# A narrower last part and smaller pieces: splitting the last tile's W4 groups 512/128 and the weight loads in a gated attention/MLP kernel

## The chip, the cores and the metric

The kernel runs on one core of a Trainium2 chip. The metric is the device time of one execution in microseconds (us); the profile's span is about 1.8 us shorter than it. Slow runs (one execution of the kernel before took 305.26 us) are left out of every comparison. Ratios are the mean time of one kernel's fast runs over that of the other's fast runs of the same rounds on the same chip, so not quite the ratio of the medians quoted beside them; each comes with a 95% interval.

The engines are called as in the profile: PE is the matrix engine, PEld its weight loads, DVE is VectorE, ACT is ScalarE, POOL is GpSimd, SP issues the DMAs; a q after the name is the engine's instruction queue.

## The reference, cut to what matters

```python
# x: (1, 2048, 640) bf16; B_w3: (640, 1728), B_w4: (1728, 640)
def reference(...):
    g = sigmoid((x * gate_w).sum(-1, keepdims=True))
    a = linear_attention(x, A_wqkv) @ A_wo            # 32 heads of 20
    x1 = x + shifted(gelu(layernorm(x) @ B_w1)) @ B_w2
    b = x1 + gelu(layernorm(x1) @ B_w3) @ B_w4
    return g * a + (1 - g) * b                        # (1, 2048, 640) bf16
```

The last step of the program is the W4 product of the last 512 rows: four chunks of 128 rows, each 640 output columns wide and 1728 deep (13 full groups of 128 and a rest of 64).

## The kernel before

An accumulator tile ("pair") is two parts of 512 float32 columns, here called banks; there are four such tiles. In W4 each chunk takes one pair. Its 640 columns are cut at 256: half 0 in the first bank, half 1 (384 columns) in the second, side by side so that VectorE can read 640 columns at once.

```python
TS = 512; LT = TS // 2; D = 640; FF = 13; NT = 4

def pair():
    return ps.tile([P, 2, 512], F32, name="pp")       # pool of 4

def w4_dst(cc, pts, hf):
    return (pts[cc][:, 0, TS - LT:TS], 0, LT) if hf == 0 else (pts[cc][:, 1, 0:D - LT], LT, D)

def w4_mm(t, cc, pts, hf, start):                     # 13 matmuls, one group
    dst, a, b = w4_dst(cc, pts, hf)
    for fc in range(FF):
        nc.tensor.matmul(dst, lhsT=st[t]["h2"][:, ...], rhs=w4_sb[:, fc, a:b], start=..., stop=...)

def w4_part(t, cc, pts, hf):                          # one half: VectorE, then a store
    src, a, b = w4_dst(cc, pts, hf)
    oc = outp.tile([P, D], BF16, name="oc")
    nc.vector.scalar_tensor_tensor(oc[:, a:b], src, omg[:, c:c + 1], st[t]["x1"][cc][:, a:b], ...)
    nc.sync.dma_start(out2[c * P:(c + 1) * P, a:b], oc[:, a:b])

def w4_tile(t):
    ...                                               # chunks 0 and 2, then the rest rows of all four
    for cc in (0, 2):
        w4_out(t, cc, pts[cc])                        # a whole chunk: VectorE 640 columns, one store
    last = t == NT - 1
    for cc, hf in ((3, 1), (1, 0), (1, 1), (3, 0)) if last else ((1, 0), (1, 1), (3, 0), (3, 1)):
        ...
        w4_mm(t, cc, pts, hf, False)
        if last and cc == 3:
            w4_part(t, cc, pts, hf)
        elif hf == 1:
            w4_out(t, cc, pts[cc])
```

The weights that the change touches come early in the program, all from SP's queue, and GpSimd gathers 128 columns of w1 from four places into `w1x`:

```python
sp.dma_start(wv_sb[:], wqkv_v[:, :, 2 * D:3 * D])
sp.dma_start(w1_sb[:], B_w1.rearrange("(c p) f -> p c f", p=P))
...                                                   # wo, w2
sp.dma_start(w3_sb[:], B_w3.rearrange("(c p) f -> p c f", p=P))
...
for g in range(4):
    nc.gpsimd.tensor_copy(w1x[:, :, 32 * g:32 * (g + 1)], w1_sb[:, :, CG * g + P:CG * (g + 1)])
```

The framework adds the waits on semaphores by itself. DMAs take their semaphores in turn out of a set of eight, so how many DMAs a program has decides which one the last store gets.

## Time and profile before

| | |
|---|---|
| time, fast runs | 266.3 and 266.91 us, profiled run 266.17 us |
| span of the profiled run | 264.4 us |
| PE busy | 259.7 us (98%) |
| last matmul's end to the end of the span | 3.70 us |

The first two parts of the page that matter are the busy times and the chain that ended last, of the kernel before (the chain's shares are by engine):

```profile
PE 259.7 (98%) x1744; PEld 162.2 (61%) x1744; DVE 139.3 (53%) x270; ACT 85.1 (32%) x126; POOL 20.2 (8%) x55
...
PE 91%; SPq 3%; DMA 3%; ACT 1%; issue 0%; DVE 0%
```

PE is the limit, and it has no pauses to win back except at the two ends. This is the timeline of the last 12 us (start, duration, engine, source line, operation, count; in brackets the idle time just before it and what ended it):

```profile
253.49 7.24 PE L479 MATMUL pp<-w_sb,h 128*128 128x384 bf16 x52
...
259.35 0.89 DVE L495 SCALAR_TENSOR_TENSOR oc<-pp,omg,x 128x640 bf16<-128x640 f32 x1 [2.60 <-PE pp L479]
260.26 0.33 SPq L497 DMA_DIRECT2D out_dram<-oc  x1
260.77 0.48 DVE L503 SCALAR_TENSOR_TENSOR oc<-pp,omg,x 128x256 bf16<-128x256 f32 x1 [0.53 <-PE pp L479]
261.28 0.33 SPq L505 DMA_DIRECT2D out_dram<-oc  x1
```

The 52 matmuls run without a break. After them stand one VectorE instruction, one store, and then 1.6 us from the store's issue to its landing, as the list of DMA issues of the last 14 us shows for the kernel before (what, from where, count, size, median us to landing):

```profile
out_dram<-oc SPq DMA_DIRECT2D x3, 160.0 KB, 1.8
out_dram<-oc SPq DMA_DIRECT2D x1, 96.0 KB, 1.6
out_dram<-oc SPq DMA_DIRECT2D x1, 64.0 KB, 1.6
```

The rest belongs to the program's closing instructions, which the views of engine work leave out. The view of their source line has them, here for the kernel before (engine, operation, count: min/median/max ns, first and last start):

```profile
L591 SPq EVENT_SEMAPHORE  x7: 17/28/28, 262.9 to 264.4; - x7
...
L591 POOLq DRAIN  x3: 78/171/1149, 203.7 to 264.0; - x3
L591 SPq DRAIN  x3: 7/7/13, 263.2 to 263.5; - x3
...
L591 POOLq EVENT_SEMAPHORE_RANGE_CLEAR  x1: 96/96/96, 263.6 to 263.6; - x1
```

SP passes its first closing check at 262.9 us, when the store has landed, and only then reaches its drain at 263.2 us. GpSimd clears the semaphores at 263.6 us (0.1 us), but its last drain starts at 264.0 us.

### The profile page before, as it was taken

Reading aid. Unit: us, or ns where it says so; the run is one execution under the profiler, and the core shown is the slowest. Engines: PE = TensorE matmul, PEld = TensorE weight load, DVE = VectorE, ACT = ScalarE, POOL = GpSimd, SP = SyncE. Lnnn points to the kernel's source line nnn. Section 1 sums busy time; section 2 is a strip of 40 time slices with the busy share of each in tenths; the row PEclk is TensorE's granted clock in tenths of the full one; section 3 lists DMA queues with packets and bytes.
Section 4 is the critical chain, followed back from the end, with each engine's and each line's share of the span. In section 5 each row is a group of like instructions: output and inputs, shape, how many; then the busy total and the mean of one; then the engine's idle time right before and its main releaser. Section 6 shows DMA issues by size and latency. Waiting matters only on the chain.

```text
span 264.4 us, 4255 instructions
## 1 busy us (share of the span) xinstructions
PE 259.7 (98%) x1744; PEld 162.2 (61%) x1744; DVE 139.3 (53%) x270; ACT 85.1 (32%) x126; POOL 20.2 (8%) x55
## 2 busy tenths in 40 slices
PE   8999999999999999999999999999999999999994
PEld 4767555788755644555667555667565667455762
DVE  1788688899858588955403464503455313112132
ACT  1555444321165636622502212312131422233000
POOL 7100010012300140001000001000001000000000
PEclk9999999999999999999999999999999999999999
DMA  7999978015673727600132000042000041100011
GB/s 202 184 211 365 377 222 318 0 43 121 128 92 68 78 51 193 207 0 2 25 74 77 25 0 2 0 99 75 26 0 2 1 99 58 44 0 2 0 59 40
DMA packets 46093, 23.61 MB, mean 89 GB/s; under 512 B 35451, under 2 KB 45435, under 8 KB 46075
## 3 DMA queue, kind: packets, MB, share of 16 engines
q1 hardware_dynamic: 45632, 22.86, 34.0%
q10 hardware_dynamic: 442, 0.49, 0.5%
q8 instruction: 13, 0.21, 0.3%
q14 instruction: 6, 0.04, 0.1%
HBM read 12.21 MB, written 2.62 MB: 56 GB/s over the span
## 4 chain that ended last, share of the span: by engine, by line
PE 91%; SPq 3%; DMA 3%; ACT 1%; issue 0%; DVE 0%
PE pp L479 22%; PE pp L460 21%; PE pp L307 8%; PE pp L413 8%; PE pp L444 8%; PE pp L341 8%; PE pp L232 8%; PE pp L190 4%; SPq L121 3%; DMA xT<-in_A_x_dram 3%; PE pp L468 1%; PE pp L488 1%; ACT m_sb L381 1%; PE pp L360 1%; PE pp L247 0%; SPq L124 0%
## 5 line engine op out<-in xcount | busy, mean ns | idle before, releaser
L460 PE MATMUL pp<-lnxT,w_sb 128*128 128x512 bf16 x260 | 60.4, 379 | 0.0
L479 PE MATMUL pp<-w_sb,h 128*128 128x256 bf16 (+1 forms) x416 | 57.9, 299 | 0.0
L462 ACT ACTIVATE h<-pp 128x1024 bf16<-128x1024 f32 (+1 forms) x28 | 26.9, 961 | 82.2 <-PE pp L460 82.2
L479 PEld LDWEIGHTS <-h 128*128 128x128 bf16 x416 | 40.3, 98 | 16.6 <-issue 1.1
L460 PEld LDWEIGHTS <-w_sb 128*128 128x128 bf16 x260 | 25.4, 98 | 26.8
L495 DVE SCALAR_TENSOR_TENSOR oc<-pp,omg,x 128x640 bf16<-128x640 f32 x15 | 12.9, 882 | 44.0 <-ACT h2x L471 21.3
L447 DVE SCALAR_TENSOR_TENSOR x<-pp,gate,x 128x640 f32<-128x640 f32 x16 | 13.9, 868 | 29.4 <-PE pp L444 29.4
L416 DVE TENSOR_TENSOR x<-pp,x_sb 128x640 f32<-128x640 f32 x16 | 13.1, 820 | 22.6 <-PE pp L413 22.6
L182 ACT ACTIVATE e<-pp 128x640 bf16<-128x640 f32 (+1 forms) x26 | 21.5, 826 | 9.6 <-PE pp L232 9.6
L444 PE MATMUL pp<-m_sb,pqT 128*128 128x320 bf16 x160 | 24.3, 299 | 0.0
L413 PE MATMUL pp<-w_sb,hsT 128*128 128x320 bf16 x160 | 23.9, 299 | 0.1
L190 PE MATMUL pp<-wk_sb,xT 128*128 128x320 bf16 (+1 forms) x160 | 22.6, 300 | 0.1
L307 PE MATMUL pp<-x_sb,pk 128*128 128x320 bf16 (+1 forms) x160 | 22.3, 300 | 0.0
L232 PE MATMUL pp<-xT,hsT 128*128 128x512 bf16 x100 | 21.7, 379 | 0.0
L307 PEld LDWEIGHTS <-pk 128*128 128x128 bf16 x160 | 18.8, 117 | 3.5
L413 PEld LDWEIGHTS <-hsT 128*128 128x128 bf16 x160 | 15.6, 98 | 8.2 <-issue 0.2
L444 PEld LDWEIGHTS <-pqT 128*128 128x128 bf16 x160 | 15.7, 98 | 7.7
L190 PEld LDWEIGHTS <-xT 128*128 128x128 bf16 x160 | 15.4, 98 | 6.4 <-DMA xT<-in_A_x_dram 0.6
L341 PE MATMUL pp<-lnxT,w_sb 128*128 128x512 bf16 x80 | 17.9, 379 | 0.0
L232 PEld LDWEIGHTS <-hsT 128*128 128x128 bf16 x100 | 11.8, 118 | 9.7
L277 POOL TENSOR_SCALAR rstd<-mv 128x4 f32<-128x4 f32 (+1 forms) x11 | 3.4, 313 | 156.5 <-DVE mv L283 156.5
L184 DVE SCALAR_TENSOR_TENSOR pk<-pp,e 128x640 bf16<-128x640 f32 x16 | 13.2, 825 | 1.7
(77 smaller groups left out, 191.6 us busy)
## 6 DMA issues: line engine op xcount, KB each, us to landing
out_dram<-oc SPq DMA_DIRECT2D x15, 160.0 KB, 1.8
w_sb<-in_B_w_dram SPq DMA_DIRECT2D x1, 2160.0 KB, 8.4
w_sb<-in_B_w_dram SPq DMA_DIRECT2D x1, 2080.0 KB, 10.0
x_sb<-in_A_x_dram SPq DMA_DIRECT2D x2, 640.0 KB, 10.7
x_sb<-in_A_x_dram SPq DMA_DIRECT2D x1, 1120.0 KB, 8.2
wo_sb<-in_A_wo_dram SPq DMA_DIRECT2D x6, 160.0 KB, 8.3
hsT<-in_A_wqkv_dram SPq DMA_DIRECT2D x1, 800.0 KB, 5.7
m_sb<-in_A_wqkv_dram SPq DMA_DIRECT2D x1, 800.0 KB, 11.5
```

The lines of the kernel that those rows point to most:

```text
L182: nc.scalar.activation(ev, src, ACT.Exp)
L184: nc.vector.scalar_tensor_tensor(dst, src, 0.0, ev, op0=ALU.max, op1=ALU.add)
L190: nc.tensor.matmul(pt[:, hf, 0:n], lhsT=xT[:, dc, c * P:(c + 1) * P], rhs=wk_sb[:, dc, hf * HD:hf * HD + n], start=(dc == 0), stop=(dc == ...
L232: nc.tensor.matmul(pt[:, t % 2, :], lhsT=wq_sb[:, dc, :].rearrange("p (m j) -> p j m", j=DC)[:, j], rhs=xT[:, dc, t * TS:(t + 1) * TS], st ...
L307: nc.tensor.matmul(pt[:, hf, 0:HD + hf], lhsT=w, rhs=x_sb[:, c, hf * HD:(hf + 1) * HD + hf], start=(c == 0), stop=(c == NCH - 1))
L341: nc.tensor.matmul(pt[:, i, :], lhsT=w, rhs=lnxT[t][:, dc, :], start=(dc == 0), stop=(dc == DC - 1))
L413: nc.tensor.matmul(pt[:, hf, 0:HD], lhsT=hsT[:, fc, 2 + c * P:2 + (c + 1) * P], rhs=w2_sb[:, fc, hf * HD:(hf + 1) * HD], start=(fc == 0), ...
L444: nc.tensor.matmul(pt[:, hf, 0:HD], lhsT=pqT[:, j, c * P:(c + 1) * P], rhs=m_sb[:, j, hf * HD:(hf + 1) * HD], start=(j == 0), stop=(j == D ...
L447: nc.vector.scalar_tensor_tensor(x1, pt[:, :, 0:HD], gate[:, c:c + 1], x1, op0=ALU.mult, op1=ALU.add)
L460: nc.tensor.matmul(pt[:, k, :], lhsT=w3_sb[:, dc, fc * P:(fc + 1) * P], rhs=lnT[:, dc, :], start=(dc == 0), stop=(dc == DC - 1))
L462: nc.scalar.activation(h2[:, 2 * i * TS:(2 * i + n) * TS], pt[:].rearrange("p h e -> p (h e)")[:, 0:n * TS], ACT.Gelu_apprx_tanh)
L479: nc.tensor.matmul(dst, lhsT=st[t]["h2"][:, fc * TS + cc * P:fc * TS + (cc + 1) * P], rhs=w4_sb[:, fc, a:b], start=start and fc == 0, stop ...
```

## The change

Its intent: the last VectorE instruction and the last store are to be narrower (128 columns in place of 256), and the early weight loads and copies are to be in finer pieces, so that their readers can start sooner. The groups of chunks 1 and 3 in the last tile become 512 and 128 columns, both wide ones first, and every group gets its own VectorE instruction and store.

```diff
-    sp.dma_start(wv_sb[:], wqkv_v[:, :, 2 * D:3 * D])
-    sp.dma_start(w1_sb[:], B_w1.rearrange("(c p) f -> p c f", p=P))
+    for a, b in ((0, 2), (2, DC)):
+        sp.dma_start(wv_sb[:, a:b, :], wqkv_v[:, a:b, 2 * D:3 * D])
+    for a, b in ((0, 2), (2, DC)):
+        sp.dma_start(w1_sb[:, a:b, :], B_w1[a * P:b * P, :].rearrange("(c p) f -> p c f", p=P))
 ...                                                  # w3 in two pieces in the same way
-    for g in range(4):
-        nc.gpsimd.tensor_copy(w1x[:, :, 32 * g:32 * (g + 1)], w1_sb[:, :, CG * g + P:CG * (g + 1)])
+    for a, b in ((0, 1), (1, 2), (2, 3), (3, DC)):
+        for g in range(4):
+            nc.gpsimd.tensor_copy(w1x[:, a:b, 32 * g:32 * (g + 1)], w1_sb[:, a:b, CG * g + P:CG * (g + 1)])
 ...
-    def w4_dst(cc, pts, hf):
-        return (pts[cc][:, 0, TS - LT:TS], 0, LT) if hf == 0 else (pts[cc][:, 1, 0:D - LT], LT, D)
+    def w4_dst(t, cc, pts, hf):
+        n = D - TS if t == NT - 1 and cc % 2 else LT
+        return (pts[cc][:, 0, TS - n:TS], 0, n) if hf == 0 else (pts[cc][:, 1, 0:D - n], n, D)
 ...                                                  # w4_part: both parts of a chunk share one oc tile
-        for cc, hf in ((3, 1), (1, 0), (1, 1), (3, 0)) if last else ((1, 0), (1, 1), (3, 0), (3, 1)):
+        for cc, hf in ((3, 1), (1, 1), (1, 0), (3, 0)) if last else ((1, 0), (1, 1), (3, 0), (3, 1)):
 ...
-            if last and cc == 3:
+            if last:
                 w4_part(t, cc, pts, hf)
```

More of the change, by code (lines that the diff above doesn't have):

```diff
@@ L145 @@
         sp.dma_start(w2_sb[32 * g:32 * (g + 1), 4, :], B_w2[CG * g + P:CG * (g + 1), :])
-    sp.dma_start(w3_sb[:], B_w3.rearrange("(c p) f -> p c f", p=P))
+    for a, b in ((0, 2), (2, DC)):
+        sp.dma_start(w3_sb[:, a:b, :], B_w3[a * P:b * P, :].rearrange("(c p) f -> p c f", p=P))
     nc.gpsimd.memset(mhalf[:], -0.5)
@@ L471, in w3_rest @@
         nc.scalar.activation(st[t]["h2x"][:], dst, ACT.Gelu_apprx_tanh)
-    def w4_dst(cc, pts, hf):
-        return (pts[cc][:, 0, TS - LT:TS], 0, LT) if hf == 0 else (pts[cc][:, 1, 0:D - LT], LT, D)
+    def w4_dst(t, cc, pts, hf):
+        n = D - TS if t == NT - 1 and cc % 2 else LT
+        return (pts[cc][:, 0, TS - n:TS], 0, n) if hf == 0 else (pts[cc][:, 1, 0:D - n], n, D)
     def w4_mm(t, cc, pts, hf, start):
-        dst, a, b = w4_dst(cc, pts, hf)
+        dst, a, b = w4_dst(t, cc, pts, hf)
         for fc in range(FF):
@@ L486, in w4_rest @@
                     rows = slice(FR * v, FR * (v + 1))
-                    dst, a, b = w4_dst(u + 2 * v, pts, hf)
+                    dst, a, b = w4_dst(t, u + 2 * v, pts, hf)
                     nc.tensor.matmul(dst, lhsT=st[t]["h2x"][rows, u * P:(u + 1) * P],
@@ L497, in w4_out @@
         nc.sync.dma_start(out2[c * P:(c + 1) * P, :], oc[:])
+    ocs = {}
     def w4_part(t, cc, pts, hf):
         c = t * CPT + cc
-        src, a, b = w4_dst(cc, pts, hf)
-        oc = outp.tile([P, D], BF16, name="oc")
+        src, a, b = w4_dst(t, cc, pts, hf)
+        if cc not in ocs:
+            ocs[cc] = outp.tile([P, D], BF16, name="oc")
+        oc = ocs[cc]
         nc.vector.scalar_tensor_tensor(oc[:, a:b], src, omg[:, c:c + 1], st[t]["x1"][cc][:, a:b],
```

## The prediction

(Stages that it and the experiments name: the key stage is the run of matmuls up to 27.2 us, the query stage the one from there to 49 us, the kv unit 30 narrow matmuls at 76.5 us.)

> **What bounds the kernel.** TensorE. The table of busy time gives PE 259.7 us of a 264.4 us span (98%); the table of stretches shows it at 100% from 10 us to 256 us, granted clock 1.00. The 4.7 us without PE work are 0.8 us at the start and 3.6 us after the last matmul (260.74 us). The chain of waits is 91% PE. No matmul waits for wv, w1 or w3 in the list of waits.
>
> **Weight loads.** One load each of wv (issued 19.5 us, landed 11.5 us later), w1 (21.9, 11.1 us) and w3 (37.7 us) becomes two; the bytes stay the same. Their first readers run at 76.4, 71.0 and 104.1 us: 35 us or more of slack. x comes before them in the queue. SP idles from 39 to 54 us. Critical part: zero.
>
> **GpSimd copies.** Four copies of 0.31 us (1.21 us from 33.05 us) become sixteen smaller ones; I estimate 2 to 4 us together, mostly fixed cost. The next GpSimd work is at 55.95 us, the copies' reader at 75.3 us. VectorE may be held up a little ("SBUF — State Buffer" of the Trainium skill says that the two share a port pair exclusively), but has 0.40 us idle per query unit there and PE does not wait for it. Critical part: zero. The instruction comparison shows four extra semaphore waits on PE, all long satisfied; at most 0.1 us in all.
>
> **The tail** alone is on the critical path. Now, after the last matmul: VectorE 128x256 0.48 us (from 260.77), store issued 261.28, landing 1.6 us later, then 1.5 us to the end of the span. The last part becomes 128 columns. The same VectorE instruction takes 0.88 us at 640 columns, 0.62 at 384 and 0.48 at 256: 1.04 ns per column plus 0.22 us, so 0.35 us at 128 (estimate) and 0.75 us at 512. Gain 0.13 us.
>
> Does the earlier work catch up in time? The two 128-column groups, 26 matmuls, last about 1.46 us at an estimated 56 ns each (in the kv unit 30 matmuls of 120 or 40 columns with their own weights took 1.43 us, 48 ns each). VectorE needs 0.75 + 0.35 us inside them, so it is ready. PE work is the same 640 columns per row chunk, PE time within 0.1 us. "TensorE: Matmul & The Clock Gate" (Back-to-back issue gap) gives 81 ns for 128 columns; then the tail would lose 0.65 us. The kv unit disagrees, so I don't expect it.
>
> The last store is halved to 32 KB, in pieces of 256 B. Landing is mostly fixed here (1.8 us at 160 KB, 1.6 us at 64 and 96 KB); I expect 1.5 to 1.7 us. Two stores issued 1.0 and 0.7 us earlier may still be in flight; little queueing.
>
> **Sum.** 0.1 to 0.2 us shorter, span 264.25 us: nothing beside the scatter between undisturbed runs (266.2, 266.3, 266.9 us). Time 266.4 us, range 265.8 to 267.2. Faster by over 2%: 0.01; within 2%: 0.97; slower: 0.02.
>
> **What would show it.** PE busy 259.7 ± 0.3 us; last VectorE part near 0.35 us; last matmul at 260.7 ± 0.2 us; landing 1.5 to 1.7 us; no PE wait for weights; sixteen copies over before 45 us.
>
> **What would make it wrong.** 128-column matmuls limited by weight loads (last matmul over 0.5 us later); the 256 B store or its predecessors delaying the landing; GpSimd's copies blocking VectorE so that PE starves of accumulator buffers; a median in the slow state (305 us seen once).

## The result

| | before | after |
|---|---|---|
| runs of the first comparison | 305.26 (slow), 266.3, 266.91, 266.48 us | 266.17, 266.23, 266.55, 266.49 us |
| median | 266.7 us of all four, the slow one with them; 266.48 us of the three fast | 266.36 us |
| ratio of fast runs | | 0.9992, interval 0.9973 to 1.0012 |
| span of the profiled run | 264.4 us | 264.5 us |

The time is as predicted: the same. The way there is not. These are the busy times and the chain of the kernel after:

```profile
PE 260.0 (98%) x1744; PEld 161.5 (61%) x1744; DVE 139.5 (53%) x271; ACT 85.2 (32%) x126; POOL 21.9 (8%) x67
...
PE 97%; ACT 1%; DVE 0%; issue 0%
```

PE is as busy as before. The last pieces of the chain of the kernel after, in order of time (start, duration, what):

```profile
253.59 5.73 PE pp L484 x26
259.32 0.02 issue
259.34 0.76 DVE oc L512
260.11 0.04 issue
260.15 1.62 PE pp L484 x26
261.77 0.03 issue
261.80 0.35 DVE oc L512
```

(The chain's larger PE share comes from the first 16 us, where it is now followed through PE instead of through the transposing loads; nothing became slower or faster by that.) In the kernel before the chain had one piece of 52 matmuls, 253.56 to 260.74 us. Here it goes from the matmuls through a VectorE instruction and back to the matmuls: PE waits for VectorE. The timeline of the kernel after says the same:

```profile
253.52 5.79 PE L484 MATMUL pp<-w_sb,h 128*128 128x512 bf16 x26
...
259.34 0.75 DVE L512 SCALAR_TENSOR_TENSOR oc<-pp,omg,x 128x512 bf16<-128x512 f32 x1 [2.05 <-PE pp L484]
260.15 1.61 PE L484 MATMUL pp<-w_sb,h 128*128 128x128 bf16 x26 [0.84 <-DVE oc L512]
...
261.80 0.35 DVE L512 SCALAR_TENSOR_TENSOR oc<-pp,omg,x 128x128 bf16<-128x128 f32 x1 [0.38 <-PE pp L484]
```

So does its list of waits (who waited, for whom, us in total, times, longest), which has no such line in the kernel before:

```profile
PE pp L484 <- DVE oc L512: 0.8, 1, 0.8
```

The first 128-column matmul waits until VectorE has read chunk 1's wide half. PE stands still for 0.84 us by the profile, and it loses more than that. The last wide matmul starts at 258.925 us and the first narrow one at 260.147 us, 1.22 us apart where 0.216 us is the pace of the wide ones: 1.00 us lost. The difference of 0.16 us is what a wide matmul lasts in the profile (0.379 us) beyond that pace (0.216 us); where another one follows at once, the two overlap and it doesn't show. The Trainium skill says in "Perfetto Trace Analysis" (Tensor Engine Instruction) that the end of a matmul in the profile is an estimate; here it means that an idle time read off the profile is too small by that much.

So the last matmul ends 1.00 us later (counted from the first query-stage matmul), and yet the span is the same. The end got shorter by as much. The DMA issues at the end of the kernel after:

```profile
out_dram<-oc SPq DMA_DIRECT2D x2, 160.0 KB, 1.8
out_dram<-oc SPq DMA_DIRECT2D x2, 128.0 KB, 1.7
out_dram<-oc SPq DMA_DIRECT2D x2, 32.0 KB, 1.4
```

The last store lands a little sooner. The closing instructions of the kernel after:

```profile
L600 SPq EVENT_SEMAPHORE  x7: 17/28/28, 262.6 to 264.4; - x7
...
L600 POOLq DRAIN  x3: 40/78/1156, 203.8 to 264.2; - x3
L600 SPq DRAIN  x3: 7/7/13, 263.7 to 264.0; - x3
...
L600 POOLq EVENT_SEMAPHORE_RANGE_CLEAR  x1: 96/96/96, 264.1 to 264.1; - x1
```

GpSimd's last drain now follows its clearing at once (264.1 and 264.2 us; before 263.6 and 264.0 us). And SP passes its first check while the last store is still on its way.

The table takes the span apart, by single instructions of the traces. It starts at the first query-stage matmul, because the time before that one changes from run to run (see the end of this document). "SP signals" is the second of SP's three closing drains, the first of them that signals another engine (GpSimd, 0.03 us later); the expectations below call it SP's first closing drain, or just its drain.

| us | before | after |
|---|---|---|
| first query-stage matmul to end of last matmul | 233.48 | 234.48 |
| to the end of the last VectorE instruction | 0.52 | 0.39 |
| to the issue of the last store | 0.03 | 0.03 |
| issue to landing | 1.56 | 1.44 |
| landing to "SP signals" | 0.41 | 0.15 |
| "SP signals" to the end | 1.18 | 0.71 |
| sum | 237.18 | 237.19 |

(The sums are taken before rounding.) Lost: 1.00 us. Won: 0.13 us at VectorE, as predicted, and 0.12 us at the landing, of which the prediction had at most 0.1 us (1.5 to 1.7 us after 1.6); and 0.26 and 0.47 us in the closing part, which it did not have.

### The profile page after: what moved, and what is told of

The parts are those of the page before. It is cut to its first block, busy times and chain, and to the rows that moved or that the text cites. A ratio compares the mean times of both kernels' runs of the same rounds, so it can differ in the third digit from the quotient of the medians.

```text
span 264.5 us, 4272 instructions
## 1 busy us (share of the span) xinstructions
PE 260.0 (98%) x1744; PEld 161.5 (61%) x1744; DVE 139.5 (53%) x271; ACT 85.2 (32%) x126; POOL 21.9 (8%) x67
## 4 chain that ended last, share of the span: by engine, by line
PE 97%; ACT 1%; DVE 0%; issue 0%
PE pp L484 22%; PE pp L464 21%; PE pp L311 8%; PE pp L194 8%; PE pp L417 8%; PE pp L448 8%; PE pp L345 8%; PE pp L236 8%; PE pp L206 1%; PE pp L472 1%; PE pp L493 1%; ACT m_sb L385 1%; PE pp L364 1%; PE pp L251 0%; DVE oc L512 0%; PE pp L383 0%
## 5 line engine op out<-in xcount | busy, mean ns | idle before, releaser
L484 PE MATMUL pp<-w_sb,h 128*128 128x256 bf16 (+3 forms) x416 | 58.0, 299 | 0.8 <-DVE oc L512 0.8
L484 PEld LDWEIGHTS <-h 128*128 128x128 bf16 x416 | 39.3, 98 | 18.8 <-issue 2.2
L500 DVE SCALAR_TENSOR_TENSOR oc<-pp,omg,x 128x640 bf16<-128x640 f32 x14 | 12.0, 881 | 41.4 <-ACT h2x L475 21.3
```

The lines of the kernel that those rows point to most:

```text
L484: nc.tensor.matmul(dst, lhsT=st[t]["h2"][:, fc * TS + cc * P:fc * TS + (cc + 1) * P], rhs=w4_sb[:, fc, a:b], start=start and fc == 0, stop ...
```

## The experiments

**Theory of the wait.** Chunk 1's narrow group accumulates in the first bank of the tile whose second bank VectorE is reading. The banks are different, but the wait is kept for the tile: in the trace the first narrow matmul waits for VectorE's semaphore. In the order of the kernel before no group followed directly on a read of its own tile, so the same wait was there (for chunk 3's last group) and long satisfied. Rivals: any reading of the accumulators holds PE up; or narrow groups are slow by themselves, as 81 ns per 128-column matmul (the skill's figure in the prediction) would have it.

**Theory of the end.** SP ends the program with five checks of two semaphores each, one after another, about 0.066 us apart. By the trace they come in the order (103, 104), (102, 105), (100, 106), (107, 109), (108, 110); the eight DMA semaphores are 100 and 102 to 108, the other two belong to VectorE and ScalarE. The last store of the kernel before has semaphore 104: all five checks wait for it, four of them still have to be made after it has landed. Four more DMAs in the kernel after (three more loads, one more store) turn it into 108, which is in the last check. And GpSimd's 0.37 us pause sits at a place in its instruction stream. Rivals: the pieces really speed up something early, or the end is shorter by chance.

All kernels computed the right result. Each of the first two sets ran on one chip, five rounds against the kernel before; the last set is one run each, and its state is therefore unknown, but its readings are of single instructions in the trace. The "sum" below is that of the table above, first query-stage matmul to the end.

One miss is common to the first four expectations: their absolute times (last matmul, span). In these traces the first query-stage matmul came at 27.89 to 28.05 us, 0.6 to 0.8 us later than in the trace of the kernel before (27.25 us), also in the run without the pieces, and nine runs of the kernel before on the same chip had spans of 264.9 to 265.6 us. So e4_free_tiles ended its last matmul at 261.53 us where 260.75 was expected, and e3_order at 261.64 where about 261.05 was, which by the letter is its rival's figure. The readings below count from the first query-stage matmul, which these four expectations didn't yet do; the ratios against the kernel before in the same rounds don't depend on it.

### e1_loads_only: the pieces without the tail

```diff
 # the kernel before, plus:
+    (wv, w1 and w3 in two loads each, sixteen GpSimd copies, as in the change)
```

> The kernel before with only the pieces of the change (wv, w1, w3 in two loads, sixteen GpSimd copies), tail as before. If the pieces are off the critical path, the last matmul ends at 260.7 to 260.8 us as before. The theory of the closing part says that the end still shortens: three more loads move the last store's semaphore from the first to the fourth of SP's five closing checks, so landing to SP's first closing drain falls from 0.41 us to about 0.2 us; and if the 0.37 us that GpSimd idles before its last drain belongs to the place in GpSimd's program, it goes too (0.03 us in the changed kernel, which has the same GpSimd program). Span 263.8 us with both, 264.2 with the checks alone. Rival: the pieces delay something or do nothing at all, span 264.4 us or more with the end as before.

Median 266.08 us against 266.78 us of the kernel before, ratio 0.9968 (0.9954 to 0.9982). First query-stage matmul to last matmul: 233.48 us, exactly as before, so the pieces speed up no stage. The last store has semaphore 107; landing to "SP signals" 0.21 us. GpSimd's pause is 0.03 us. Sum 236.47 us, 0.70 us less than before. The pieces are worth 0.7 us, and all of it lies after the last store's issue: 0.02 us at the landing, 0.20 at the checks, 0.48 at GpSimd.

### e2_tail_only: the tail without the pieces

```diff
 # the change, minus:
-    (the pieces)
```

> The change without its pieces: only the last tile's 512/128 split. If the wait for VectorE comes from the tail's order alone, PE again idles 0.84 us before the first 128-column matmul and the last matmul ends at 261.75 us. One more store than before puts the last store's semaphore into the second closing check, so landing to drain is about 0.35 us, not 0.15. Span 264.7 us, or 265.1 if the GpSimd gap of 0.37 us belongs to the old GpSimd program. Rival (the pieces have a part in the wait): wait under 0.5 us.

Median 267.32 us, ratio 1.0021 (1.0008 to 1.0033): slower, clear of noise but far under 2%. First query-stage to last matmul 234.48 us, as in the kernel after: the wait is the tail's. Semaphore 105, landing to "SP signals" 0.34 us, GpSimd's pause 0.37 us. Sum 237.86 us, 0.68 us more than before. The two halves of the change, +0.68 and -0.70 us, cancel.

### e3_order: the narrow groups swapped

```diff
-        for cc, hf in ((3, 1), (1, 1), (1, 0), (3, 0)) if last else ...
+        for cc, hf in ((3, 1), (1, 1), (3, 0), (1, 0)) if last else ...
```

> The changed kernel with the two 128-column groups swapped: chunk 3's before chunk 1's. If PE waits because chunk 1's two groups share one accumulator tile, which VectorE is still reading, then chunk 3's group runs first without a wait (its tile's reader was done 2 us earlier) and chunk 1's group waits only for the rest: 0.2 to 0.3 us of idle instead of 0.84, last matmul at about 261.05 us, span about 263.75 us. Rival (any VectorE read of the accumulators stops PE, or small groups are slow by themselves): idle 0.8 us or last matmul at 261.6 us or later, span 264.4 us.

Median 265.95 us, ratio 0.9969 (0.9957 to 0.9982). First query-stage to last matmul 233.75 us: 0.27 us lost in place of 1.00 (0.12 us of idle by the profile), because chunk 3's group (13 matmuls at 56 ns, 0.73 us) runs while VectorE reads chunk 1. It reads the accumulators all the while, so a read as such doesn't hold PE up.

### e4_free_tiles: the same order, other tiles

The columns of the pairs of chunks 0 and 2 that nobody uses take the two narrow groups. VectorE is done with those tiles 4 us earlier.

```diff
     def w4_dst(t, cc, pts, hf):
         n = D - TS if t == NT - 1 and cc % 2 else LT
+        if hf == 0 and n != LT:
+            return pts[cc - 1][:, 0, 0:n], 0, n
         return ...
```

> The changed kernel, same order, but the two 128-column groups accumulate in unused columns of the tiles of chunks 0 and 2, which VectorE has finished with 4 us before. If sharing a tile is the cause, no wait remains although VectorE still reads the accumulators at the same time: PE idle under 0.1 us, last matmul at 260.75 us, span 263.45 us, 0.4% faster than before (ratio 0.996). Rival (the hardware or the weight loads hold PE): last matmul at 261.6 us or later, span 264.4 us.

Median 265.79 us, ratio 0.9958 (0.9945 to 0.9970), the fastest of the versions run in rounds. First query-stage to last matmul 233.48 us, as in the kernel before: the whole 1.00 us is back. The timeline of this run's tail:

```profile
254.30 7.24 PE L486 MATMUL pp<-w_sb,h 128*128 128x512 bf16 x52
...
260.12 1.08 DVE L514 SCALAR_TENSOR_TENSOR oc<-pp,omg,x 128x512 bf16<-128x512 f32 x2 [2.05 <-PE pp L486]
261.57 0.35 DVE L514 SCALAR_TENSOR_TENSOR oc<-pp,omg,x 128x128 bf16<-128x128 f32 x1 [0.38 <-PE pp L486]
```

One piece of 52 matmuls again, 7.24 us as in the kernel before, with VectorE at work beside it. Order, widths and instructions are those of the change; only the tile of two groups differs. That settles the cause: the shared tile. The narrow matmuls stand 55.8 ns apart here, start to start.

### e5_pad12: only twelve more GpSimd instructions

```diff
     nc.gpsimd.memset(kvT[:], 0.0)
+    for _ in range(12):
+        nc.gpsimd.memset(mhalf[:], -0.5)
```

> The kernel before with nothing but twelve more instructions on GpSimd: repeated clears of a small constant, early in its program. Same loads, same copies, same tail. If the 0.37 us that GpSimd idles before its last drain (and that drain's 0.17 us instead of 0.03) belongs to how long GpSimd's program is, both go, and the run is about 0.45 us shorter than before (ratio 0.9983); SP's closing checks stay as before, 0.41 us from landing to its drain. Rival (the gap went because of the copies or of the split loads): gap 0.37 us stays, ratio 1.000.

Median 266.14 us against 266.65 us of the kernel before in this set, ratio 0.9985 (0.9971 to 0.9999). GpSimd's pause is 0.03 us and its last drain 0.03 us; landing to "SP signals" stays 0.41 us, the matmuls stay at 233.48 us. Sum 236.69 us, 0.49 us less than before. Twelve instructions without any use win half a microsecond, so it was not the copies.

### e6_split_only: only the three loads in two pieces

```diff
 # the kernel before, plus:
+    (wv, w1 and w3 in two loads each; GpSimd's four copies as before)
```

> The kernel before with only the three loads split in two, GpSimd's program as before. If the order of the closing checks is what counts, landing to SP's drain falls from 0.41 to about 0.14 us because the last store's semaphore is now in the fourth check, and GpSimd's gap of 0.37 us stays: 0.25 us shorter than before, ratio 0.999. Rival (splitting loads speeds up or slows down the early stages): the query stage starts earlier or later against the key stage's last matmul, which is not expected.

Median 266.31 us, ratio 0.9990 (0.9975 to 1.0005). Semaphore 107, landing to "SP signals" 0.21 us, 0.20 us less than before. (The 0.14 us expected is the time to the drain ahead of it, here 0.14 us; to that drain the kernel before took 0.34 us, not 0.41.) The expectation that GpSimd's pause stays was right in size and wrong in place: the pause ahead of the last drain had gone from 0.371 to 0.026 us, but a pause of 0.382 us now stood one instruction earlier, ahead of the clearing:

```profile
L594 POOLq DRAIN  x3: 50/78/1144, 204.4 to 264.4; - x3
...
L594 POOLq EVENT_SEMAPHORE_RANGE_CLEAR  x1: 96/96/96, 264.3 to 264.3; - x1
```

With w1 in two loads GpSimd has one more semaphore instruction, 72 in place of 71 instructions. Everything behind it moves by one place, and the pause doesn't. Sum 236.84 us, 0.34 us less than before: 0.20 at the checks, 0.02 at the landing, 0.12 because the last drain took 0.050 in place of 0.171 us.

### e7_free_shift: three more loads on top of e4_free_tiles

```diff
-    for a, b in ((0, 2), (2, DC)):
+    for a, b in ((0, 1), (1, 2), (2, 3), (3, 4), (4, DC)):
         sp.dma_start(w3_sb[:, a:b, :], ...)
```

> The version with the 128-column groups in the free tiles, with w3 loaded in five pieces instead of two. Three more loads move the last store's semaphore from the fifth closing check to the first. Everything up to the last store's landing stays; landing to SP's drain grows from about 0.14 to 0.41 us, so 0.26 us longer than with two pieces (ratio 0.9968 where that had 0.9958). Rival: the number of loads has nothing to do with the end, landing to drain stays at 0.14 us.

Ratio 0.9976 (0.9962 to 0.9990), median 266.0 us. The last store has semaphore 103, in the first check; landing to "SP signals" is 0.39 us where e4_free_tiles has 0.15, and nothing else moved: sum 236.42 against 236.17 us. Finer loading costs 0.25 us here, only through the semaphore's turn.

### e8_after_again: the change beside the others

No edit: the kernel after once more.

> The changed kernel again, beside the others and the kernel before on one chip. By the sum of the parts (0.84 us of PE wait and 0.17 us of exposed drain of the matmuls lost; about 0.25 us at VectorE and the landing, 0.26 us at the checks and 0.47 us at GpSimd gained) ratio 0.9995 to 1.0005; PE idles 0.84 us before the first 128-column matmul again.

Median 266.38 us, ratio 0.9999 (0.9979 to 1.0019). Sum 237.19 us, to the hundredth that of the first trace. The span was 265.9 us: 1.4 us more than in the first trace, all of it before the first query-stage matmul.

### e9_pad2 and e10_pad4: where GpSimd's pause sits

```diff
     nc.gpsimd.memset(kvT[:], 0.0)
+    for _ in range(2):                  # e10_pad4: range(4)
+        nc.gpsimd.memset(mhalf[:], -0.5)
```

> The kernel before with two more instructions on GpSimd early in its program. In the kernel before GpSimd stalls 0.37 us between its clearing of the semaphores and its last drain; with one more instruction (split loads alone) the same 0.38 us stood one instruction earlier, ahead of the clearing; with twelve more it was nowhere. If the stall sits at a fixed place in GpSimd's instruction stream, two more instructions move it one further: about 0.37 us between GpSimd's second closing semaphore instruction and the drain ahead of the clearing, and 0.03 us at the two later places. Rival (it goes with what GpSimd did before): the stall stays ahead of the last drain or is gone.

> As the run with two, with four more instructions. The fixed place then falls to the first closing semaphore instruction, which GpSimd waits at for SP anyway: no stall over 0.1 us among GpSimd's closing instructions, the part from SP's first closing drain to the end of the span 0.47 us shorter than in the kernel before, everything else as before. Rival: stall of 0.37 us anywhere in GpSimd's closing part.

With two more, the pause is 0.42 us and stands ahead of the drain before the clearing (0.207 us long in place of 0.078); the later gaps are 0.03 us. The sum stays 237.18 us. The closing line of e9_pad2 in the trace, two of its entries:

```profile
L593 POOLq DRAIN  x3: 34/207/1144, 204.1 to 264.5; - x3
L593 POOLq EVENT_SEMAPHORE_RANGE_CLEAR  x1: 96/96/96, 264.4 to 264.4; - x1
```

With four more there is no pause anywhere in the closing part, and the sum is 236.70 us. The same entries of e10_pad4:

```profile
L593 POOLq DRAIN  x3: 34/77/1144, 204.0 to 264.0; - x3
L593 POOLq EVENT_SEMAPHORE_RANGE_CLEAR  x1: 96/96/96, 263.8 to 263.8; - x1
```

Over 71, 72 and 73 instructions the pause moved forward by as many places as were put in; with 75 that place would be GpSimd's first closing instruction, where it waits for SP anyway, and no pause is seen. It is tied to a place in the instruction stream.

### e11_order_384 and e12_wide_old_order: order or width?

```diff
 # e11_order_384: the change with the old widths
-        n = D - TS if t == NT - 1 and cc % 2 else LT
+        n = LT
 # e12_wide_old_order: the change with the old order, chunk 1 read and stored whole
-        for cc, hf in ((3, 1), (1, 1), (1, 0), (3, 0)) if last else ...
+        for cc, hf in ((3, 1), (1, 0), (1, 1), (3, 0)) if last else ...
-            if last:
+            if last and cc == 3:
```

> The changed kernel's order and separate stores with the old widths of 256 and 384 columns. If the wait of PE is VectorE's reading of the shared tile, its length follows VectorE's instruction: 0.62 us at 384 columns in place of 0.75, so PE idles about 0.71 us in place of 0.84. After the last matmul 2.95 us to the end in place of 2.71 (last VectorE part 0.48, landing 1.56). Rival (the wait belongs to narrow groups): no idle with 256 columns.

> The changed kernel with its widths of 512 and 128 columns but the old order (chunk 1's narrow group before its wide one, chunk 1 read and stored whole). No wait of PE over 0.1 us, because no group follows a read of its own tile; last matmul where the kernel before has it. VectorE's 0.88 us over chunk 1 now ends after chunk 3's last group of 13 matmuls (0.73 us), so the last VectorE part starts about 0.17 us after the last matmul in place of 0.03. Rival (width is the cause): PE idles 0.8 us or loses it on the narrow matmuls.

With 256 and 384 columns in the new order PE waits too, and by as much less as VectorE's instruction is shorter:

```profile
258.35 0.62 DVE L512 SCALAR_TENSOR_TENSOR oc<-pp,omg,x 128x384 bf16<-128x384 f32 x1 [1.18 <-PE pp L484]
259.02 3.00 PE L484 MATMUL pp<-w_sb,h 128*128 128x256 bf16 x26 [0.71 <-DVE oc L512]
```

0.71 us after an instruction of 0.62 us, where the change had 0.84 after 0.75. With 512 and 128 columns in the old order the matmuls take 233.48 us, so there is no wait; the last VectorE part starts 0.11 us after the last matmul (0.17 expected), and its store is issued 0.20 us after it, not 0.03, behind chunk 1's store. Sum 236.58 us. The order is the cause of the wait; the width only sets its length.

## Why the prediction was right, and where its steps were not

The predicted time (266.4 us, range 265.8 to 267.2) held: 266.36 us. The change is within 2%, as given at 97%. That is right for the sum, but two of its steps were wrong, by 1.00 and by 0.73 us in opposite directions, and nearly cancelled. That the time came out so close to the number given is therefore luck: with the loss alone (+0.68 us, e2_tail_only) it would have stood at about 267.2 us, the upper edge of the range. That the change stayed within 2% (5.3 us) is not luck; neither error could have upset it.

- **"PE work is the same 640 columns per row chunk, PE time within 0.1 us" and "last matmul at 260.7 ± 0.2 us".** PE busy was as said (260.0 us), the last matmul wasn't: 261.76 us. What failed is the step "does the earlier work catch up in time?": it asked whether VectorE would be ready for PE's results, and not whether PE would have to wait for VectorE. It did, for 0.84 us of idle and 1.00 us in all. This could be seen in the diff: VectorE now reads chunk 1's wide half as soon as it is done, and the next group of matmuls writes the same tile. The prediction counted four extra waits on PE and took them all for long satisfied. Its own sign of being wrong, "last matmul over 0.5 us later", came true, but not by the weight loads that it named.
- **"then 1.5 us to the end of the span".** This was carried over as a constant. It fell from 1.59 us (0.41 + 1.18) to 0.86 us (0.15 + 0.71). The missing term has two parts, 0.26 us at SP's checks and 0.47 us at GpSimd.
- **"Weight loads: critical part zero" and "GpSimd copies: critical part zero".** For what they were reasoned about (readers, slack, the shared port) this is right: 233.48 us of matmuls with and without the pieces, and VectorE's instructions beside the copies (0.43 and 1.22 us) are no longer than before (0.43 and 1.23 us), so the trace doesn't show VectorE held up. But they won 0.70 us at the end, nearly all of it by changing the number of DMAs and of GpSimd instructions. Both steps looked for an effect where the work is done and not where the program ends.
- **The tail's terms.** VectorE 0.35 us at 128 columns: measured 0.35. At 512 columns 0.75: measured 0.75. Gain 0.13: measured 0.13. Landing 1.5 to 1.7 us: 1.44, slightly below. "DMA: Bandwidth & Descriptors" (Anatomy of one DMA) gives a fixed part of about 2.0 us for a DMA of the GpSimd path; on this path 32 KB take 1.44 us in all, and the size dependence is small here too (1.8 us at 160 KB). Pieces of 256 B cost nothing visible at this size (1.44 us, against 1.56 us for 64 KB in pieces of 512 B).
- **128-column matmuls at 56 ns against 81 ns.** Measured 55.7 ns start to start in the kernel after, each with its own weights. The estimate of 56 ns was right; the page's sustained figure doesn't hold for these narrow groups.
- **Sixteen copies in 2 to 4 us, over before 45 us.** They took 2.82 us and ended at 34.4 us, as this line of the kernel after shows:

```profile
31.58 2.82 POOL L178 COPY w1x<-w_sb 128x32 bf16<-128x32 bf16 x16 [24.04 <-DMA w_sb<-in_B_w_dram]
```

What stays open is why GpSimd pauses at that place. An instruction fetch is a possible reason: "Runtime: NRT & Kernel Launch" (Instruction fetch mechanics) says that instructions are refilled in blocks through a DMA queue that the sequencer drives. In the traces with the pause (before, e2, e6, e9) the instruction queue has an 8 KB packet 0.1 to 0.3 us after the end of the span; in those without, none stands there: with four more instructions it stands at 206.2 us, about 1 us after GpSimd's last computing instruction, and in all nine traces with twelve more at 73.6 to 75.0 us. So the packet goes by the count of GpSimd's instructions, as the pause does. That fits, but the packet starts after the pause is over, so the pause can't be the wait for that packet's bytes, and no run shows which it is.

## What to carry to other kernels

When PE is told to write into a tile that another engine is about to read, look at the order of groups by tile, not by bank or column: put groups of other tiles, or unused columns of tiles long read, between the read and the next write (here worth 1.00 us of a 264 us kernel for two added lines, or 0.73 us for swapping two groups). When a tuned kernel changes by less than a microsecond, take the closing part apart before crediting the edit: which semaphore the last store has and where the instruction streams end were worth up to 0.7 us here, as much as the tail itself. A change that comes out neutral may be two effects: run its parts alone.

## What the Trainium skill lacked or had wrong

- "TensorE: Matmul & The Clock Gate" (Back-to-back issue gap): the sustained figure of 81 ns for 128-column matmuls with their own weight loads is too high for this chain; 55.7 ns were measured over 26 of them, which is what the same page gives for isolated ones (about 56 ns).
- The same page, on the clock gate, is borne out and explains a part of the scatter: it says that the array starts at half clock and that the moment of the change varies by run. In the run of e4_free_tiles the 320-column matmuls up to 6.6 us stood 267 ns apart and later ones 136 ns, and the first query-stage matmul came at 28.05 us; in the run of before none was slow, and it came at 27.25 us. In e8_after_again a gap of 1.07 us among the key-stage matmuls came on top of slow ones (28.70 us). But in six other traces (e1, e5, e6, e7, e10, e12) none was slow and the first query-stage matmul still came 0.27 to 0.70 us later than in before; there PE stood waiting for loads (0.78 us at 6.5 us in e1_loads_only). Measured from that matmul on, the two traces of the kernel after agree within 0.01 us.
- No page tells of the framework's closing part: five checks of two semaphores each, the eight of the DMAs among them, one after another, about 0.066 us apart. Landing to signal measured 0.41 and 0.39 us with the last store in the first check, 0.34 in the second, 0.21 in the fourth, 0.15 in the fifth.
- "Runtime: NRT & Kernel Launch" (Instruction fetch mechanics) calls the cost of a block's boundary mostly hidden. GpSimd paused 0.37 to 0.42 us at a fixed place of its stream near the end, where nothing hid it (whether it is the fetch stays open).
- "Perfetto Trace Analysis" tells that matmul ends are estimates, but not what follows for a wait: 0.84 us of idle in the profile cost 1.00 us of matmul starts.
